# Queues laid by a list scheduler inside the kernel, and gate columns copied with the values

## The chip, the cores and the metric

The kernel runs on one core of one Trainium2 chip. Its time is the device time of one execution in microseconds (us). TensorE (PE) multiplies matrices; VectorE (DVE), ScalarE (ACT) and GpSimd (POOL) work on elements; SyncE (SP) issues loads and stores. Each engine takes its instructions strictly from the front of its own queue, and an instruction that has to wait holds up all that stand behind it.

## The reference

Three stages follow each other, all in float32, for 2 batches of 768 rows.

```
# 1: attention, 8 heads of width 64, window of 96 keys plus 8 global keys
scores = q @ k.T / 8 + bias(head, distance);  scores = where(keep, scores, -1e9)
a = softmax(scores);  x = a @ v                      # heads side by side: 512 wide
# 2: four causal attention experts of width 64, two of four chosen per row
logits = x @ w_gate;  top 2 of 4;  w = softmax over the two chosen
ye = softmax(causal(x wq[e] (x wk[e]).T / 8)) @ (x wv[e]) @ wo[e]
x = sum over chosen e of w[e] * ye
# 3: mixing along the rows (rank 32), then a channel MLP
u = x + (U V mixed over the rows);  out = u + relu(u @ w_ch1) @ w_ch2      # 512 -> 2048 -> 512
```

Four of the weights come as float64 (U, V, w_ch1 and w_ch2) and are narrowed to float32 on the chip with integer operations.

## The kernel before, in words

Stage 1 is cut into 12 pairs of units (`a_pair`), six for each batch, and stage 2 into 12 more (`d_pair`), one for three of the row groups of two experts. A pair goes through `score` (PE, into two banks `S`), `soft` (DVE: the row minimum of the scaled and masked scores, L245; ACT: the exponential with its row sum, L256), `rec` (DVE: reciprocals of the sums, L263 to L266; POOL: the probabilities `pr` times them, L269), `turn` (PE transposes into the banks `T`, `U` or `acc`, L199, and a copy to a tile `pt`, by ACT or DVE in turn), and `values` (PE, into the bank `X`), whose result is copied by ACT as a high part and subtracted by DVE as a low part (`xT`).

The pairs run in positions r = -1 to 23. In position r, PE scores pair r+1, then multiplies the values of pair r-1, then transposes pair r. Between these stand fillers: `c_heads` and `c_values` project x to the experts' queries, keys and values (L362, L363), and `w_fold` multiplies `wo` into a block of w_ch1 (L568). All fillers write into one bank, `acc`, which has one buffer, so each has to be emptied before the next may start. Projections of values put 256 columns of `v` and 4 of gate logits `lg` into that bank; ACT copies `v` (L389) and DVE copies `lg` (L390). From position 6 on the transposes use only `T` and `U`.

A narrowed piece takes an ACT instruction (L83), a POOL instruction that clears all but the sign (L84) and two DVE instructions, here called joins (L89, L90). `w_load` does this for w_ch1 and `w2_load` for w_ch2, whose low part `w2l` DVE then subtracts (L75).

After the pairs comes a seam: `y_turn`, `y_mix` and `y_out` mix along the rows. `y_out` adds the mixed part to `zT` (DVE, L626), copies the sum as a high part (ACT) and subtracts the low part (DVE). The banks `S` are then given to `h`, so the first `h` matmul also waits for all four additions of batch 0. Stage 3 (`M`) is four halves of 16 steps: in each step PE makes a block `h` of the hidden layer, ACT and DVE make its two parts (L649, L650), and PE multiplies the block before it with w_ch2 into three banks. In the first 13 steps DVE still narrows w_ch2.

The order on every engine is the order in which the program is written: `in_order` at the end of `run` chains each instruction to the one before it on its engine. `run` sets what is written when: the table `fill` gives the fillers of each position, `at` and `stages` put loads, conversions and scalings at named points ("dma", "mid", "mid2", "end") of a position, and `position` writes one position out.

Of the kernel before, what the change touches and what calls it, by code (L numbers as in the profile page):

```python
# [9 lines left out]
F32 = mybir.dt.float32  # L10
# [8 lines left out]
P = 128  # L19
# [27 lines left out]

class Pair:
# [6 lines left out]
class Body:  # L55
# [36 lines left out]
    def raw_tile(self):  # L92
        return self.cv.tile([P, 2 * DM], I32, tag="wr", name=self.uid("cr"), bufs=3)
# [107 lines left out]
    def moved(self, t, w, g):  # L201
        pt = self.soft_.tile([P, 512], F32, tag="pt", name=self.uid("pt"), bufs=4)
        (self.hi_dve if g % 2 else self.hi_act)(pt[:, :w], t[:, :w])
        return pt


    def a_load_qk(self, J, first=False):
        nc, a, raw = self.nc, self.a, self.araw
        b, j = divmod(J, NJ)
        qr = raw.tile([P, S], F32, tag="qr", name=self.uid("qr"), bufs=2)  # L210
        kx = raw.tile([P, KW], F32, tag="kx", name=self.uid("kx"), bufs=2)
# [139 lines left out]
    def stacks(self, pool):  # L351
        t = lambda tag, shape, dt: pool.tile(shape, dt, tag=tag, name=self.uid(tag))
        qk = [t(f"qk{n}", [P, 2, S], F32) for n in range(2)]
        v = t("v", [P, NB, E * D], F32)
        g = t("g", [P, NB, E], F32)
        lg = t("lg", [P, NB, E], F32)
        return *qk, v, g, lg
# [20 lines left out]
    def c_values(self, b, t):  # L378
        nc = self.nc
        v, g, lg = self.st[b][2:5]  # L380
# [24 lines left out]
    def gate(self, b):  # L405
        nc = self.nc
        g, lg = self.st[b][3:5]
        sh = [P, NB, E]
        cnt = self.small.tile(sh, F32, tag="cnt", name=self.uid("cnt"), bufs=2)
        c = self.small.tile(sh, F32, tag="cmp", name=self.uid("cmp"), bufs=2)  # L410
        m = self.small.tile([P, NB], F32, tag="gm", name=self.uid("gm"), bufs=2)
# [18 lines left out]
    def causal(self, pool):  # L430
        nc = self.nc
        self.cm = pool.tile([P, 640], F32, name="cm")
        nc.vector.memset(self.cm, 0.0)
# [112 lines left out]
    def w_load(self, f):  # L546
        raws, ts = [], []
        for c in range(0, 4, 2):
# [4 lines left out]
            yield  # L553
# [3 lines left out]
        self.w1[f] = [t.bitcast(F32).rearrange("p (c n) -> p c n", c=2) for t in ts]  # L557
        for r, t in zip(raws, ts):
            self.narrow_join(r, t)
            yield  # L560
# [71 lines left out]
    def M(self, side):  # L632
# [34 lines left out]
        def store(m, t):  # L667
            b, th = halves[m]
            o = self.soft_.tile([P, DM], F32, tag="pt", name=self.uid("o"), bufs=4)
# [93 lines left out]

    def open(self, name, side="left", bufs=1, space=None):
        kw = {"space": space} if space is not None else {"side": side}
        cm = self.tc.tile_pool(name=self.uid(name), bufs=bufs, **kw)
        pool = cm.__enter__()
        self.cms[id(pool)] = cm
        return pool

    def close(self, *pools):
        for p in pools:
            self.cms.pop(id(p)).__exit__(None, None, None)


    def run(self, dense):
        nc = self.nc
        mark = len(nc.cur_bb.bb.instructions)
        self.cms = {}
# [49 lines left out]
        if not dense:  # L829
            for J in range(2, 2 * NJ):  # L830
                r = 3 * (J // 2) + J % 2
                at(r - 2, "dma", self.a_load_qk, J)
                at(r - 2, "end", self.a_scale, J)
                at(r, "dma", self.a_load_v, J)
        for kc in range(4):
            stages(lambda kc=kc: self.wall_load(kc), (kc, "dma"), (kc + 1, "mid"), (kc + 2, "end"))
        uv = [self.u_load, lambda: self.v_load(0), lambda: self.v_load(1)]
        for n, g in enumerate(uv):
            r = 6 + n
            stages(g, (r, "dma"), (r + 1, "mid"), (r + 1, "end"), (r + 2, "mid"), (r + 2, "end"))  # L840
# [9 lines left out]
        fill[6] = [], [], H0[:1]  # L850
        fill[7] = H0[1:2], H0[2:3], []
        fill[8] = H0[3:4], V0[:1], []
        fill[9] = V0[1:2], V0[2:3], []
        fill[10] = V0[3:4], V0[4:5], []
        fill[11] = V0[5:], [], []
        fill[12] = G0[:1], G0[1:2], []
        fill[13] = G0[2:3], G0[3:], []
        fill[14] = H1[:1], H1[1:2], H1[2:3]
        fill[15] = H1[3:], V1[:1], V1[1:2]
        fill[16] = V1[2:3], W[0:1], V1[3:4]  # L860
        fill[17] = V1[4:5], V1[5:], W[1:2]
        fill[18] = G1[:1], G1[1:2], W[2:3]
        fill[19] = G1[2:3], G1[3:], W[3:4]
        fill[20] = [], W[4:5], []
        fill[21] = [], W[5:6], []
        fill[22] = [], W[6:7], []
        at(11, "end", self.gate, 0)
        at(17, "mid2", self.gate, 1)
        for f in range(DFF // CW):
            r = 16 + f  # L870
            stages(lambda f=f: self.w_load(f), (r - 2, "mid2"), (r - 2, "end"), (r - 1, "mid"), (r - 1, "end"))
# [17 lines left out]
        aux.setdefault((14, "dma"), []).insert(0, middle)  # L889
# [14 lines left out]
        def position(r):  # L904
# [4 lines left out]
            full = f1 or f2 or f3 or not pv  # L909
            if nx:  # L910
                nx.score()
            if cur:
                cur.rec()
# [3 lines left out]

            def mins(n):
                for _ in range(n):
                    if next(gen, 1):  # L920
                        break
# [14 lines left out]
            def moved():  # L936
                if outs:
                    outs.pop(0)()

            if not full:  # L940
                mins(6)
                exps(4)
                pv.out_hi()
# [206 lines left out]
```

## Time and profile before

| | us |
|---|---|
| median of 3 runs | 510.98 |
| lowest and highest of them | 509.60, 513.28 |
| the profiled execution's own time | 514.29 |
| its span, first to last instruction | 511.6 |
| PE busy | 459.1 |
| DVE, ACT and POOL busy | 249.3, 201.3, 110.3 |
| mean granted clock of PE | 0.964 |

The profiled execution is one run, 3.3 us above the median of the others; 2.7 us of its time lie outside the span. Matmuls are pipelined and their ends are modelled, so a busy PE need not be PE at its peak. A name such as `acc` stands for all buffers of a tile. L12 is line 12 of the kernel before.

### The profile page before, as it was taken

How to read it: one execution, taken by the hardware profiler on the slowest of the kernel's cores; microseconds unless marked ns; L12 is line 12 of the kernel's file. 1: busy time of each engine (PE TensorE's matmuls, PEld its weight loads, DVE VectorE, ACT ScalarE, POOL GpSimd, SP SyncE). 2: the span in 40 equal slices, each digit the busy share in tenths (PEclk: the TensorE clock that was granted, in tenths of full speed). 3: DMA queues.
4: the chain of work that ended last, by engine and by line, in shares of the span. 5: the costliest groups of instructions: out<-in, count | busy, mean ns of one | idle time of the engine just before them, and what ended most of it. 6: DMA issues, size and time to landing. Idle time of an engine off the chain costs nothing. (4 is left out here: it accounts for less than half of the span.)

```text
span 511.6 us, 7948 instructions
## 1 busy us (share of the span) xinstructions
PE 459.1 (90%) x2916; PEld 384.9 (75%) x2916; DVE 249.3 (49%) x720; ACT 201.3 (39%) x547; POOL 110.3 (22%) x210
## 2 busy tenths in 40 slices
PE   5898799787999977987985999899999999999995
PEld 4676689676887766865774887788888888888883
DVE  4597647556436566465657688941111211111111
ACT  6686557643334444425443444521111111111111
POOL 3577326322231323313421122200000000000000
PEclk9798799989999999998997999999999999999999
DMA  8444622100041221222222333310000100010002
GB/s 301 167 156 156 201 96 77 38 1 1 5 162 41 85 84 41 83 82 85 83 82 83 123 124 124 124 42 21 0 1 0 63 1 0 1 62 1 0 1 69
DMA packets 17648, 36.66 MB, mean 72 GB/s; under 512 B 2560, under 2 KB 6400, under 8 KB 17600
## 3 DMA queue, kind: packets, MB, share of 16 engines
q1 hardware_dynamic: 15728, 34.49, 20.8%
q10 hardware_dynamic: 1872, 1.58, 0.9%
q8 instruction: 25, 0.41, 0.3%
q14 instruction: 23, 0.19, 0.1%
HBM read 32.91 MB, written 3.15 MB: 70 GB/s over the span
## 5 line engine op out<-in xcount | busy, mean ns | idle before, releaser
L256 ACT ACTIVATE pr<-pr,nm 128x256 f32<-128x256 f32 (+4 forms) x144 | 77.4, 540 | 61.3 <-DVE nm L245 61.3
L650 DVE SCALAR_TENSOR_TENSOR pr<-h,pr 128x384 fp32r<-128x384 f32 x64 | 35.5, 554 | 128.3 <-ACT pr L649 128.3
L269 POOL TENSOR_SCALAR pr<-pr,rec 128x256 f32<-128x256 f32 (+4 forms) x144 | 72.0, 521 | 120.2 <-DVE rec L266 66.6
L649 ACT ACTIVATE pr<-h 128x384 fp32r<-128x384 f32 x64 | 31.4, 490 | 136.4 <-PE h L363 136.3
L84 POOL TENSOR_SCALAR cr<-cr 128x512 f32<-128x512 f32 (+2 forms) x35 | 25.4, 733 | 92.6 <-ACT ct L83 76.2
L362 PE MATMUL acc<-xT,wh 128*128 128x384 f32 x128 | 36.2, 365 | 5.5 <-ACT qk L69 5.0
L89 DVE SCALAR_TENSOR_TENSOR cr<-cr 128x512 int32<-128x512 int32 (+2 forms) x35 | 27.8, 794 | 15.1 <-POOL cr L84 15.1
L241 PE MATMUL S<-kx,qr 64*128 64x256 f32 (+1 forms) x192 | 29.3, 448 | 5.8 <-ACT qr L224 4.5
L568 PE MATMUL acc<-ct,woT 128*128 128x256 f32 x128 | 30.4, 392 | 4.3 <-DVE lg L390 2.3
L199 PE MATMUL T<-ident,pr 128*128 128x128 f32 x164 | 28.6, 292 | 5.6 <-POOL pr L269 5.5
L199 PE MATMUL U<-ident,pr 128*128 128x128 f32 x148 | 26.4, 295 | 7.6 <-ACT pt L69 5.6
L245 DVE CUSTOM_DVE_ANT_0 pr<-S,dw 128x256 f32<-128x256 f32 x80 | 29.2, 419 | 6.8 <-PE S L241 5.5
L568 PEld LDWEIGHTS acc<-ct,woT 128*128 128x128 f32 x128 | 24.5, 197 | 8.5 <-DVE lg L390 2.8
L362 PEld LDWEIGHTS acc<-xT,wh 128*128 128x128 f32 x128 | 23.6, 199 | 7.8 <-ACT qk L69 5.8
L241 PEld LDWEIGHTS S<-kx,qr 64*128 64x128 f32 x192 | 20.7, 229 | 11.5 <-ACT qr L224 4.8
L90 DVE SCALAR_TENSOR_TENSOR ct<-ct,cr 128x512 int32<-128x512 int32 (+2 forms) x35 | 26.8, 767 | 1.8
L199 PEld LDWEIGHTS U<-ident,pr 128*128 128x128 f32 x148 | 19.1, 150 | 11.3 <-POOL pr L269 5.6
L72 DVE COPY pt<-T 128x512 f32<-128x512 f32 x26 | 17.9, 688 | 19.6 <-PE T L199 19.5
L199 PEld LDWEIGHTS T<-ident,pr 128*128 128x128 f32 x164 | 20.2, 148 | 9.5 <-POOL pr L269 8.4
L256 ACT ACTIVATION_READ_ACCUMULATOR pr<-pr,nm 128x1 f32 x144 | 27.2, 189 | 0.0
L245 DVE CUSTOM_DVE_ANT_0 pr<-S,cm 128x512 f32<-128x512 f32 (+3 forms) x48 | 24.5, 554 | 3.2 <-PE S L241 3.2
L362 PE MATMUL acd<-w2h,pr 128*128 128x512 f32 x64 | 25.3, 395 | 0.0
(266 smaller groups left out, 1053.7 us busy)
## 6 DMA issues: line engine op xcount, KB each, us to landing
cr<-in_w_dram SPq DMA_DIRECT2D x32, 512.0 KB, 3.6
kx<-in_kx_dram SPq DMA_DIRECT2D x7, 464.0 KB, 5.4
v<-in_v_dram SPq DMA_DIRECT2D x8, 384.0 KB, 3.1
qr<-in_q_dram SPq DMA_DIRECT2D x7, 384.0 KB, 4.1
va<-in_va_dram SPq DMA_DIRECT2D x8, 320.0 KB, 3.5
cr<-in_wall_dram SPq DMA_DIRECT2D x4, 386.0 KB, 5.4
out_dram<-o SPq DMA_DIRECT2D x12, 128.0 KB, 1.7
out_dram<-o ACTq DMA_DIRECT2D x12, 128.0 KB, 1.7
```

What stands on the lines that cost most here:

```text
L84: nc.gpsimd.tensor_scalar(hi.bitcast(F32), hi.bitcast(F32), 0.0, -0.0, op0=ALU.mult, op1=ALU.add)
L89: nc.vector.scalar_tensor_tensor(lo, lo, 29, hi, op0=ALU.logical_shift_right, op1=ALU.bitwise_or)
L90: nc.vector.scalar_tensor_tensor(t, t, 3, lo, op0=ALU.logical_shift_left, op1=ALU.bitwise_or)
L199: self.nc.tensor.transpose(t[:, k * P : (k + 1) * P], s, self.ident)
L241: self.nc.tensor.matmul(sp[:, h, :], q[s], k[s], start=True, stop=True)
L245: self.nc.vector.tensor_tensor_reduce(out=out, in0=sp, in1=mask, scale=scale, scalar=start, op0=ALU.add, op1=ALU.min, accum_out=nm)
L256: self.nc.scalar.activation(pr[:, h, :], pr[:, h, :], AF.Exp, bias=nm[h], scale=-1.0, accum_out=den[:, k, h : h + 1])
L269: nc.gpsimd.tensor_scalar(pr[:, h, :], pr[:, h, :], rec[:, k, h : h + 1], 0.0, op0=ALU.mult, op1=ALU.add)
L362: mm(out, lh, rh, start=first, stop=False), mm(out, lh, rl, start=False, stop=False),
L568: nc.tensor.matmul(ac[:, p, :], self.woT[:, kc, p * P : (p + 1) * P], w1[kc // 2][:, kc % 2, :], start=kc == 0, stop=kc == 3)
L649: nc.scalar.activation(hh, hp, AF.Relu)
L650: nc.vector.scalar_tensor_tensor(hl, hp, 0.0, hh.bitcast(F32), op0=ALU.max, op1=ALU.subtract)
```

## The change

PE keeps the order in which the program is written. The other engines and the queue of loads get an order that a list scheduler computes inside the kernel: `Order.before` reads from the operands which instruction needs which, adds what a buffer's next use and a closed pool need, and keeps PE's order; `Order.length` gives each instruction a nominal length; `Order.queues` goes through the program in simulated order and always takes, among the instructions that could start first, the one with the longest way to the end behind it. `in_order` then chains each engine's queue in that order.

Beside it: the values' copy takes 260 columns at once, by ACT and DVE in turn, and the gate reads its logits from the last four of them; the gate counts with one comparison of all pairs; `cm` is cleared on POOL; raw tiles, `qr` and `kx` get one more buffer, and `pt` is split in two tags of two; loads are written a position earlier; and the fillers of positions 6 to 19 move to about one position earlier.

```diff
-        return self.cv.tile([P, 2 * DM], I32, tag="wr", name=self.uid("cr"), bufs=3)
+        return self.cv.tile([P, 2 * DM], I32, tag="wr", name=self.uid("cr"), bufs=4)
...
+    def length(self, i, e):
...
+        if i.opcode == "DMACopy":
+            return 450, 0, n * outs[0].ap[0][1] * 4
...
+        if e == "Activation":
+            return 150 + 0.87 * n + (120 if len(outs) > 1 else 0), 0, 0
+        if e == "DVE":
+            return (80 + 1.04 * n if i.opcode == "ISA" else 190 if n <= 64 else 150 + 1.06 * n), 40, 0
+        return (130 if n <= 64 else 230 + 0.88 * n), 60, 0
...
+        pe = [k for k, e in enumerate(self.eng) if e == "PE"]
+        for a, b in zip(pe, pe[1:]):
+            self.after[b].add(a)
+
+    def queues(self):
...
+        for _ in range(n):
+            t, e = min((min(max(free[e], ready[k]) for k in s), e) for e, s in open_.items() if s)
+            k = max((k for k in open_[e] if max(free[e], ready[k]) <= t), key=lambda k: (way[k], -k))
+            open_[e].discard(k)
+            line[e].append(k)
+            end = free[e] = t + self.cost[k]
...
-        def out():
-            nc.scalar.activation(v[:, t, :], ac[:, :256], AF.Copy)
-            nc.vector.tensor_copy(lg[:, t, :], ac[:, 256:260])
-        return out
+        return lambda: (self.hi_dve if t % 2 else self.hi_act)(v[:, t, :], ac)
...
-        for e in range(E):
-            le = lg[:, :, e : e + 1].to_broadcast((P, NB, E))
-            if e:
-                nc.vector.tensor_tensor(c[:, :, :e], lg[:, :, :e], le[:, :, :e], ALU.is_ge)
-            nc.vector.tensor_tensor(c[:, :, e:], lg[:, :, e:], le[:, :, e:], ALU.is_gt)
-            nc.vector.tensor_reduce(cnt[:, :, e : e + 1], c, axis=AX.X, op=ALU.add)
+        nc.vector.tensor_tensor(over[:, :, :, 0, :], other, own, ALU.is_gt)
+        nc.vector.tensor_tensor(over[:, :, :, 1, :], other, own, ALU.is_equal)
+        nc.vector.tensor_tensor(over[:, :, :, 1, :], over[:, :, :, 1, :], self.earlier.unsqueeze(1).to_broadcast(full), ALU.mult)
+        nc.vector.tensor_reduce(cnt.unsqueeze(3), over.rearrange("p t e k n -> p t e (k n)"), axis=AX.X, op=ALU.add)
...
-        fill[6] = [], [], H0[:1]
-        fill[7] = H0[1:2], H0[2:3], []
-        fill[8] = H0[3:4], V0[:1], []
...
-        fill[19] = G1[2:3], G1[3:], W[3:4]
...
+        fill[6] = [], H0[:1], H0[1:2]
+        fill[7] = H0[2:3], H0[3:], []
+        for n in range(3):
+            fill[8 + n] = V0[2 * n : 2 * n + 1], V0[2 * n + 1 : 2 * n + 2], []
...
+        fill[18] = G1[2:3], G1[3:], W[2:3]
+        for n in range(4):
+            fill[19 + n] = [], W[3 + n : 4 + n], []
...
-        last = {}
-        for i in self.nc.cur_bb.bb.instructions[mark:]:
-            e = i.engine
-            if e in last:
+        ins = [
+            (n, i) for n, i in enumerate(self.nc.cur_bb.bb.instructions)
+            if n >= mark and (Order.aps(i.outs) or Order.aps(i.ins))]
+        for queue in Order(self, ins).queues().values():
+            for a, b in zip(queue, queue[1:]):
                 self.tc.add_manual_dep(
-                    i, last[e].name,
+                    b, a.name,
                     mybir.DependencyInfo(mybir.DependencyClass.NoSync, mybir.DependencyReason.DATA), reason="order")
-            last[e] = i
```

DVE's queue where position 10 begins: the copies of position 9's last transposes (`pt`), then the minima of the pair scored in position 10 (`ISA`, with `dw` as the mask). Before:

```order
L390 COPY lg_113<-acc_1293 128x4
L72 COPY pt_1320<-T_1313 128x512
L75 TENSOR_TENSOR vs<-ct_1156,vs 32x384
L89 SCALAR_TENSOR_TENSOR cr_1057<-cr_1057 96x384
L90 SCALAR_TENSOR_TENSOR ct_1290<-ct_1290,cr_1057 96x384
L263 TENSOR_SCALAR rec_1339<-den_1235 128x8
L264 RECIPROCAL rec_1339<-rec_1339 128x8
L245 ISA pr_1365,nm_1367<-S_1329,dw 128x256
```

The same place in the change:

```order
L416 TENSOR_SCALAR rec_1366<-den_1249 128x8
L417 RECIPROCAL rec_1366<-rec_1366 128x8
L225 COPY pt_1303<-T_1295 128x512
L225 COPY v_111<-acc_1309 128x260
L225 COPY pt_1335<-T_1328 128x512
L398 ISA pr_1377,nm_1379<-S_1341,dw 128x256
```

The joins of `V` and the subtraction of its low part are gone from here to earlier in the queue, the reciprocals stand ahead of the copies, and the values' copy includes the gate columns.

DVE's queue at the seam: the low part `zs` of the mixed rows, the additions to `zT`, the subtractions `y00l` and `y01l`, and the narrowing of w_ch2. Before:

```order
L75 TENSOR_TENSOR zs_2989<-S_2917,zs_2989 32x256
L75 TENSOR_TENSOR wol<-cr_2887,woh 128x1024
L89 SCALAR_TENSOR_TENSOR cr_2889<-cr_2889 128x512
L90 SCALAR_TENSOR_TENSOR ct_2966<-ct_2966,cr_2889 128x512
L626 TENSOR_TENSOR zT_98<-zT_98,S_2916 128x384
L75 TENSOR_TENSOR y00l<-zT_98,y00h 128x384
L626 TENSOR_TENSOR zT_98<-zT_98,S_2916 128x384
L75 TENSOR_TENSOR y00l<-zT_98,y00h 128x384
L626 TENSOR_TENSOR zT_98<-zT_98,S_2917 128x384
L75 TENSOR_TENSOR y01l<-zT_98,y01h 128x384
L626 TENSOR_TENSOR zT_98<-zT_98,S_2917 128x384
L75 TENSOR_TENSOR y01l<-zT_98,y01h 128x384
```

In the change:

```order
L242 SCALAR_TENSOR_TENSOR cr_2868<-cr_2868 128x512
L228 TENSOR_TENSOR wpl<-acc_2933,wph 128x2x256
L243 SCALAR_TENSOR_TENSOR ct_2945<-ct_2945,cr_2868 128x512
L228 TENSOR_TENSOR zs_2968<-S_2896,zs_2968 32x256
L242 SCALAR_TENSOR_TENSOR cr_2948<-cr_2948 128x512
L783 TENSOR_TENSOR zT_98<-zT_98,S_2895 128x384 x2
L228 TENSOR_TENSOR w2l_3014<-ct_2945,w2h_3013 128x512
L783 TENSOR_TENSOR zT_98<-zT_98,S_2896 128x384 x2
L228 TENSOR_TENSOR y00l<-zT_98,y00h 128x384 x2
```

`wol` and the first piece's joins stand further ahead, the four additions come in two couples with one subtraction of w_ch2 between them, and the subtractions `y01l` have moved far back.

DVE's queue in the first steps of stage 3 in the change: `pr` is the second part of a hidden block, `z` the low part of batch 1's rows.

```order
L807 SCALAR_TENSOR_TENSOR pr_3044<-h_3037,pr_3044 128x384
L228 TENSOR_TENSOR w2l_3078<-ct_2980,w2h_3077 128x512
L243 SCALAR_TENSOR_TENSOR ct_3019<-ct_3019,cr_2983 128x512
L242 SCALAR_TENSOR_TENSOR cr_3022<-cr_3022 128x512
L243 SCALAR_TENSOR_TENSOR ct_3083<-ct_3083,cr_3022 128x512
L228 TENSOR_TENSOR w2l_3117<-ct_3019,w2h_3116 128x512
L242 SCALAR_TENSOR_TENSOR cr_3086<-cr_3086 128x512
L228 TENSOR_TENSOR w2l_3163<-ct_3083,w2h_3162 128x512
L228 TENSOR_TENSOR z_3069<-T_3070,z_3068 128x512
L807 SCALAR_TENSOR_TENSOR pr_3095<-h_3088,pr_3095 128x384
```

Three pieces of w_ch2 get their low part between the first two hidden blocks; in the kernel before, one does.

## Rows read from the trace of the kernel before

**Rows 1.** The page's first part: busy us, share of the span, instructions.
```profile
PE 459.1 (90%) x2916; PEld 384.9 (75%) x2916; DVE 249.3 (49%) x720; ACT 201.3 (39%) x547; POOL 110.3 (22%) x210
```
**Rows 2.** Windows by stage: length, busy us (instructions) by engine, clock, DMA share, GB/s.
```profile
51.84:255.80 203.96, 176.93 (x1392) 148.93 (x1392) 118.33 (x402) 98.88 (x286) 62.53 (x114) 0.96 0.24 72
255.80:277.27 21.47, 13.39 (x118) 11.06 (x117) 13.64 (x24) 8.27 (x18) 4.84 (x7) 0.92 0.30 98
277.27:326.99 49.72, 47.52 (x223) 39.38 (x224) 39.48 (x60) 23.47 (x47) 10.65 (x12) 0.97 0.35 117
```
**Rows 3.** PE's waits: instruction, what ended them, us in total, times, longest us.
```profile
PE acc L362 <- DVE lg L390: 6.6, 4, 2.1
PE h L362 <- DVE zT L626: 6.1, 1, 6.1
PE U L199 <- ACT pt L69: 5.6, 4, 2.8
PE T L199 <- POOL pr L269: 5.5, 6, 2.9
PE acc L362 <- ACT qk L69: 5.0, 3, 2.5
...
PE acc L568 <- DVE lg L390: 2.3, 2, 1.8
PE acc L362 <- DVE w2l L75: 2.1, 3, 0.9
PE acc L568 <- DVE qk L72: 2.0, 2, 1.0
PE U L199 <- POOL pr L269: 2.0, 4, 0.8
```
**Rows 4.** Timeline of position 10: start, us, engine, line, operation [idle before <-releaser].
```profile
95.45 0.55 DVE L89 SCALAR_TENSOR_TENSOR cr<-cr 96x384 int32<-96x384 int32 x1
...
96.83 0.37 DVE L245 CUSTOM_DVE_ANT_0 pr<-S,dw 128x256 f32<-128x256 f32 x1
...
97.31 0.51 ACT L256 ACTIVATE pr<-pr,nm 128x256 f32<-128x256 f32 x1 [2.94 <-DVE nm L245]
...
99.64 0.60 PE L199 MATMUL T<-ident,pr 128*128 128x128 f32 x4
...
101.73 0.36 ACT L389 ACTIVATE v<-acc 128x256 f32<-128x256 f32 x1
...
102.13 0.16 DVE L390 COPY lg<-acc 128x4 f32<-128x4 f32 x1 [1.54 <-ACT v L389]
...
102.35 0.39 PE L362 MATMUL acc<-wh,xT 128*128 128x260 f32 x1 [2.11 <-DVE lg L390]
```
**Rows 5.** Sum over windows at clock 0.50: 45.02:48.43, 58.67:65.5, 103.04:106.46, 126.94:130.35, 239.58:242.99.
```profile
sum 20.48, PE 19.64 PEld 17.01 DVE 5.71 ACT 8.01 POOL 5.91; mean PE 3.93 PEld 3.40 DVE 1.14 ACT 1.60 POOL 1.18
```
**Rows 6.** Timeline of the seam.
```profile
268.69 1.23 DVE L75 TENSOR_TENSOR wol<-cr,woh 128x1024 fp32r<-128x1024 f32 x1
...
269.32 1.12 POOL L84 TENSOR_SCALAR cr<-cr 128x512 f32<-128x512 f32 x1 [1.99 <-issue]
269.84 1.16 DVE L89 SCALAR_TENSOR_TENSOR cr<-cr 128x512 int32<-128x512 int32 x1
...
271.63 0.55 DVE L626 TENSOR_TENSOR zT<-zT,S 128x384 f32<-128x384 f32 x1
...
276.47 0.55 DVE L626 TENSOR_TENSOR zT<-zT,S 128x384 f32<-128x384 f32 x1
```
**Rows 7.** Timeline of PE in stage 3: first matmul of steps 1, 12 and 13.
```profile
284.43 0.42 PE L362 MATMUL h<-y00h,wph 128*128 128x384 f32 x1
...
326.99 0.34 PE L362 MATMUL h<-y00h,wph 128*128 128x384 f32 x1
...
330.13 0.34 PE L362 MATMUL h<-y00h,wph 128*128 128x384 f32 x1
```
**Rows 8.** The first join: count, shortest, median and longest ns, first and last start.
```profile
L89 DVE SCALAR_TENSOR_TENSOR cr<-cr x35: 349/689/1156, 75.6 to 333.3; 128x512 int32<-128x512 int32 x32, 96x384 int32<-96x384 int32 x2, 128x192 int32<-128x192 int32 x1
```

More of the change, by code (lines that the diff above doesn't have):

```diff
@@ L431, in causal @@
         nc = self.nc
+        self.earlier = pool.tile([P, E, E], F32, name="earlier")
+        nc.gpsimd.memset(self.earlier, 0.0)
+        for e in range(1, E):
+            nc.gpsimd.memset(self.earlier[:, e, :e], 1.0)
         self.cm = pool.tile([P, 640], F32, name="cm")
-        nc.vector.memset(self.cm, 0.0)
+        nc.gpsimd.memset(self.cm, 0.0)
         nc.gpsimd.affine_select(
@@ L839, in run @@
             r = 6 + n
-            stages(g, (r, "dma"), (r + 1, "mid"), (r + 1, "end"), (r + 2, "mid"), (r + 2, "end"))
+            stages(g, (r, "dma"), (r + 1, "mid"), (r + 2, "a"), (r + 2, "mid"), (r + 3, "a"))
         at(7, "end", self.causal, const)
@@ L916, in position @@
             gen = nx.soft() if nx else iter(())
[L918 to L921, printed above, removed]
+            if not full:
+                next(gen, None), next(gen, None)
+            if cur:
+                cur.rec()
+            for _ in gen:
+                pass
+            if not full:
+                do(r, "a")
             def exps(n):
@@ L934, in turn, with moved, filler, out @@
                         outs.append(turns.pop(0)())
-            def moved():
-                if outs:
-                    outs.pop(0)()
+            def moved(n=1):
+                for _ in range(n):
+                    if outs:
+                        outs.pop(0)()
+            def filler(fs):
+                return [fn() for fn in fs]
+            def out(ev):
+                for e in ev:
+                    e()
             if not full:
-                mins(6)
-                exps(4)
-                pv.out_hi()
+                exps(6)
+                if pv:
+                    pv.out_hi()
                 turn(2)
                 moved()
-                mins(1)
-                moved()
-                turn(1)
-                mins(99)
-                exps(2)
-                pv.out_lo()
+                exps(99)
+                if pv:
+                    pv.out_lo()
                 moved()
@@ L954, in position @@
                 moved()
+                turn(1)
                 do(r, "mid")
-                exps(99)
+                do(r, "mid2")
+                moved()
                 do(r, "end")
                 return
-            mins(99)
-            exps(4)
+            exps(2)
+            do(r, "sign")
+            do(r, "a")
+            exps(3)
             if pv:
@@ L1058, in turn1 @@
         def turn1(n):
-            z = [self.soft_.tile([P, 512], F32, tag="pt", name=self.uid("z"), bufs=4) for x in "hl"]
+            z = [self.soft_.tile([P, 512], F32, tag=f"pt{x}", name=self.uid("z"), bufs=2) for x in range(2)]
             self.y_turn(1, 2 * n, z, self.bank("TU"[n % 2]))()
```

233 lines of the change are left out of this document (172 added, 61 removed).

## Prediction

> **What bounds the kernel now.** I began with the page's busy times: TensorE (PE) is busy for 90% of the span and the next, VectorE, for 49% [rows 1]. So the kernel ends when PE ends, and a change that leaves PE's instructions as they are can only win what PE spends waiting or at half clock. The table of stages says where that is [rows 2]. The long middle, positions 6 to 22 with attention, the second stage and all filler, lasts 204 us with 27.0 idle. The seam between the second stage and the last is 21.5 us with 8.1 idle. The first stretch of the last stage is 49.7 us with 2.2 shown idle, and there VectorE (DVE) is busy for 39.5 us, the one place where PE has a rival for the bound. Behind 327 us a step of that stage takes 3.14 [rows 7], and I count nothing there.
>
> The list of PE's waits then says what ends them [rows 3]. Three kinds carry nearly all. Filler matmuls wait for their only accumulator bank to be emptied: 6.6 and 5.0 before `acc` matmuls of the projections, 2.3 and 2.0 before the folds, 15.9 together. Transposes wait for a copy out of their bank or for GpSimd's (POOL) normalised rows: 5.6, 5.5 and 2.0, 13.1 together. The first `h` waits once for 6.1. None of these engines is full; what they owe PE stands behind something else in their own queue.
>
> One position shows how [rows 4]. While PE is at the next pair's scores, DVE is at two joins of a matrix that is needed much later, the first at 95.45, and its first minimum starts at 96.83. So ScalarE's exponentials start late, at 97.31, the copy of `v`, queued behind all eight, starts at 101.73, the copy of `lg`, which reads the same bank, at 102.13, and the next group into `acc` at 102.35, after 2.11 us of waiting. From 103.04 on the granted clock is 0.50.
>
> The clock is the second half of the cost. Five stretches at 0.50, the lower of the two levels, 1.2 GHz, lie between 45 and 243 us, and PE is busy in them for 19.64 us [rows 5]. At 2.4 GHz the same work takes half, so 9.8 us are lost. The one at 103.04 begins 0.7 us after the wait shown in rows 4 ended; I take the others to have the same cause.
>
> **The change, part by part.** PE has as many instructions as before, in the order in which the program is written. Positions 6 to 18 get their filler about one place earlier, so its matmuls cost the same; what changes is the queues that serve PE.
>
> *Accumulator waits.* Of 15.9 us I take 11 back. In the first place shown, minima now follow the last copy directly, without joins ahead of them, and `v` with the gate columns is one copy instead of a copy on ScalarE and a second on DVE. Eight transposes lie between two fillers, and the second four of them alone took 0.60 at 99.64. That covers a copy of 0.36 which is at the head of its queue, but not one that has to wait for an exponential (0.51) first, so I don't take all. Bounds: 5 (only the waits of the kind in rows 4 go) and 15.9.
>
> *Transpose waits.* Of 13.1 I take 7, since half is behind a queue (the copy to `pt` placed behind exponentials) and half is GpSimd's own pace, which no order changes. Bounds 2 and 13.1.
>
> *Clock.* With these waits gone, most of the five stretches go: 6 of 9.8. Bounds 0 and 9.8.
>
> *Seam.* DVE does the `wol` subtraction (1.23), a join (1.16) and its second half (0.69) before the first `zT` addition, then alternates additions with subtractions that each wait for ScalarE; the last addition starts at 276.47 [rows 6], and PE's first `h`, after its 6.1 of waiting, at 277.27, where the stage begins [rows 2, 3]. Between the start of the first addition and the end of the last lie 5.4 us, of which the four additions themselves are 2.2. Now the additions stand together ahead of the subtractions, so most of the other 3.2 goes, and the 1.23 of `wol` is done earlier; one join and one `w2l` subtraction (priced as the 0.69 half) still stand in the way. 3.2 + 1.2 − 0.7 is 3.7, and I take 4, since the chance of a shorter join beside an idle GpSimd is on this side; bounds 2 and 5.
>
> *First pass of the last stage.* From 284.43 to 326.99 are eleven steps, 42.56 us, against 3.14 for a step once nothing is in its way (326.99 to 330.13) [rows 7]: 8.0 too long. Part of that is PE's own side work, which stays, and 2.1 is shown as waiting for `w2l` [rows 3]. The joins now run up to three pieces ahead, with four raw buffers instead of three. I take 3; bounds 0 and 5.
>
> *Edits at nothing.* Twelve `lg` copies of 0.16 go; six `v` copies move from ScalarE to DVE; the gate has 12 DVE instructions instead of 19. In the middle stage DVE is busy for 118 of 204 us and ScalarE for 99 [rows 2], and that idle time covers them; their worth is counted in the accumulator waits. The `cm` mask and the new `earlier` tile go to GpSimd's start, where it waits for the first loads anyway. Loads are issued earlier, but SyncE's queue has w1 loads in front of late `v` and `va` loads; those are needed a position later. If one came late, the next values would wait for its landing; PE's list has no wait for a load in this stage today.
>
> *What comes back.* Shorter positions leave each pair's chain (minima, exponentials, reciprocal, normalising, transposes) less slack. The nearest row is a transpose's wait for GpSimd, 5.5 over 6 times, 0.9 each. If each of the 17 positions from 6 to 22 got one more it would be 15; if none, 0. I take 4, nearer to none: minima and exponentials of a pair take 4.9 (96.83 to 101.73), and a position lasts 12.0 on average now (204 over 17) and 10.6 with 24 us gone, so the rest of the chain keeps some 5.7.
>
> Sum: 11 + 7 + 6 + 4 + 3 − 4 = 27. The first five attention positions, which have no filler, are left at nothing. The span goes from 511.6 to 484.6; the profiled run was 514.3, 2.7 more than its span, and the median of the runs is 511.0, 3.3 less than that run. So 487.3 for a run like the profiled one, **484 us** for the median. With all best ends the sum is 49 (462 us), with all worst ends −6 (517).
>
> **Rivals.**
> *Queues frozen on wrong lengths, slower.* The order is fixed from nominal lengths, with PE at full clock. Place: ScalarE's and DVE's queues in positions 6 to 22, where copies for PE now stand between exponentials. If PE comes later than laid down, a copy waits at the head of its queue, the exponentials behind it wait too, the next pair's transposes come late, and PE falls to half clock again. Price of one: 2.8, the longest wait of transposes for `pt` [rows 3], and 2.0, half of a mean stretch at 0.50 (20.48 over five) [rows 5], 4.8 together. It takes 32 us to turn 484 into over 516, so it decides from 7 of the 17 positions on; with eight, 522 us. For it: five positions pay such a price today with a fixed order. Against it: a later PE also delays what feeds on it, so the order mostly stays right.
>
> *Conversions collide, a smaller gain.* Joins and sign-clearing instructions are pulled forward side by side. A join beside GpSimd's sign clearing took 1.16, and that one 1.12 [rows 6]; the median over all 35 joins is 0.69 [rows 8]. If all 32 wide joins paid the difference of 0.47, DVE would have 15 us more, most of it where PE waits for DVE, in the folds and the first pass. With 13 of it on the path: 497 us. In the Trainium skill, "SBUF — State Buffer", section "Who interferes with whom", a VectorE instruction with two SBUF inputs contends with a GpSimd instruction that reads SBUF, which speaks against putting both kinds of work forward together. By that rule the nominal lengths are too short wherever the two meet, and the 1.16 beside 1.12 agrees with it; that the median join met nothing in this trace is why I give it little.
>
> *Nothing happens.* PE is 90% busy, its order is fixed, and the waits just move: 511 us.
>
> **How the numbers follow.** Forecast, 464 to 495 us: 0.70. Collisions, 495 to 505: 0.14. Nothing, 506 to 516: 0.08. Frozen queues, over 516: 0.08. A measurement tells about 1% (5 us) from no change, so faster 0.84, same 0.08, slower 0.08. The range takes in the first two and stops at the third: 464 to 506, leaving out some 0.16 above and a few hundredths below.
>
> **What would show it.** In the new profile PE's waits before `acc` should total under 6 us and those of transposes under 8; the granted clock should be 0.50 in at most two stretches between 45 and 250 us; the first `h` should come within 3 us of the last `S` matmul; the eleven steps should take under 40 us. With 24 of the 27 ahead of it, the last stage begins near 253 instead of 277. I am wrong if PE's waits keep their total and only change their names, or if DVE's joins grow towards 1.1 us on average.

## The result, and the profile after

The changed kernel takes 465.8 us (median of four runs, 465.5 to 466.5) against 511.5 for the kernel before (509.6 to 513.3): ratio 0.911, 95% interval 0.907 to 0.915. It is faster, by more than I said: 45.7 us where the forecast had 27 (484 us). The profiled run took 465.9 us and its span is 464.1, against 511.6: 47.5 us to account for.

From here on, L numbers are lines of the kernel whose trace is shown. The page's first part of the kernel after (busy us, share of the span, instructions):

```profile
PE 442.0 (95%) x2916; PEld 375.7 (81%) x2916; DVE 244.6 (53%) x699; ACT 201.1 (43%) x541; POOL 120.7 (26%) x215
```

PE has the same 2916 instructions and 17.1 us less busy time than in [rows 1]; as its work has not changed, most of this has to be clock (12.7 is worked out below). Its idle time fell from 52.5 to 22.1, the other 30.4.

Windows of the kernel after by stage (length, busy us and instructions of PE, PEld, DVE, ACT and POOL, granted clock, DMA share, GB/s); the second to fourth answer to [rows 2], cut at the same instructions of PE, the first is everything ahead of position 6:

```profile
0.00:49.23 49.23, 39.94 (x345) 29.93 (x345) 40.70 (x166) 38.20 (x133) 36.31 (x85) 0.97 0.75 256
49.23:219.65 170.42, 166.34 (x1391) 142.25 (x1391) 115.99 (x382) 97.14 (x277) 67.04 (x111) 1.00 0.25 78
219.65:235.21 15.56, 13.17 (x119) 11.07 (x117) 10.50 (x18) 9.82 (x21) 5.71 (x8) 1.00 0.32 101
235.21:279.34 44.13, 44.13 (x223) 38.36 (x224) 42.89 (x72) 25.78 (x49) 11.65 (x12) 1.00 0.41 132
```

Against [rows 2] the middle lost 33.5 us (204.0 to 170.4), the seam 5.9, the first pass of the last stage 5.6; ahead of position 6 it is 2.6 (51.84 to 49.23), and behind the twelfth step 0.2 more (184.6 to 184.8). The sum is 47.5, rounded. In the middle PE's idle time went from 27.0 to 4.1 and its clock from 0.96 to 1.00. In the first pass PE is now never idle, and VectorE is busy for 42.9 of 44.1: what was a rival for the bound is close to being it.

PE's waits in the kernel after (instruction, what ended them, us, times, longest):

```profile
PE U L352 <- POOL pr L422: 2.0, 2, 1.5
PE acc L513 <- ACT qk L222: 1.9, 3, 0.9
PE h L513 <- ACT y01h L222: 1.3, 1, 1.3
...
PE acc L513 <- ACT v L222: 0.8, 2, 0.4
PE T L352 <- POOL pr L422: 0.5, 2, 0.3
PE acc L513 <- DVE v L225: 0.5, 1, 0.5
PE acc L513 <- DVE qk L225: 0.4, 1, 0.4
PE acc L725 <- DVE qk L225: 0.4, 1, 0.4
```

The projections' and folds' waits before `acc` (L513, L725) add up to 4.0, where the rows of [rows 3] that I counted had 15.9; transposes into U and T have 2.5 in these rows and 0.4 in a smaller one, from 13.1. The wait for `lg` is gone with its copy, that for `zT` has become 1.3 for `y01h`, that for `w2l` is gone. The longest wait of PE in the middle is now 0.9.

The same place of a position as [rows 4], from the kernel after (start, us, engine, line, operation, idle before and releaser):

```profile
87.20 0.69 DVE L225 COPY pt<-T 128x512 f32<-128x512 f32 x1 [0.44 <-PE T L352]
88.39 0.42 DVE L398 CUSTOM_DVE_ANT_0 pr<-S,dw 128x256 f32<-128x256 f32 x1 [0.49 <-POOL pr L422]
...
88.86 0.51 ACT L409 ACTIVATE pr<-pr,nm 128x256 f32<-128x256 f32 x1 [1.43 <-DVE nm L398]
...
92.69 0.60 PE L352 MATMUL T<-ident,pr 128*128 128x128 f32 x4
...
93.29 0.36 ACT L222 ACTIVATE v<-acc 128x260 f32<-128x260 f32 x1
...
93.70 0.39 PE L513 MATMUL acc<-wh,xT 128*128 128x260 f32 x1 [0.41 <-ACT v L222]
```

PE's scores of this pair start at 87.10, the first minimum follows at 88.39, 1.3 later; before it was 94.04 and 96.83, 2.8 later, with a subtraction and two joins of a conversion between. The copy of `v` still stands behind all eight exponentials, so nothing put it at the head of its queue; the exponentials are just done 1.5 us sooner, and 2.11 us of waiting have become 0.41.

### The profile page after: what moved, and what is told of

Its sections match the earlier page's. It is cut to its first block, busy times and chain, and to the rows that moved or that the text cites. A ratio compares the mean times of both kernels' runs of the same rounds, so it can differ in the third digit from the quotient of the medians.

```text
span 464.1 us, 7933 instructions
## 1 busy us (share of the span) xinstructions
PE 442.0 (95%) x2916; PEld 375.7 (81%) x2916; DVE 244.6 (53%) x699; ACT 201.1 (43%) x541; POOL 120.7 (26%) x215
## 4 chain that ended last, share of the span: by engine, by line
PE 78%; ACT 8%; POOL 5%; DVE 4%; issue 3%; DMA 1%; ACTq 0%; DVEq 0%; POOLq 0%
PE h L513 10%; PE acc L513 9%; PE acd L513 7%; PE S L394 6%; PE acc L725 6%; ACT pr L409 5%; PE h L514 5%; POOL pr L422 4%; PE acc L514 4%; PE X L513 4%; PE X L652 4%; PE T L513 4%; PE acd L514 4%; PE U L513 3%; PE U L352 2%
## 5 line engine op out<-in xcount | busy, mean ns | idle before, releaser
L422 POOL TENSOR_SCALAR pr<-pr,rec 128x256 f32<-128x256 f32 (+4 forms) x144 | 78.8, 567 | 93.5 <-DVE rec L419 68.2
L237 POOL TENSOR_SCALAR cr<-cr 128x512 f32<-128x512 f32 (+2 forms) x35 | 27.4, 788 | 49.3 <-ACT ct L236 38.8
L513 PE MATMUL acc<-xT,wh 128*128 128x384 f32 x128 | 34.4, 349 | 1.9 <-ACT qk L222 1.9
L394 PE MATMUL S<-kx,qr 64*128 64x256 f32 (+1 forms) x192 | 25.6, 402 | 4.8 <-ACT qr L377 4.5
L725 PE MATMUL acc<-ct,woT 128*128 128x256 f32 x128 | 29.1, 380 | 0.4 <-DVE qk L225 0.4
L236 ACT ACTIVATE ct<-cr 128x512 f32<-128x512 f32 (+2 forms) x35 | 22.9, 658 | 14.0 <-PE acc L725 10.9
L352 PE MATMUL T<-ident,pr 128*128 128x128 f32 x164 | 26.3, 279 | 0.9 <-POOL pr L422 0.5
L725 PEld LDWEIGHTS acc<-ct,woT 128*128 128x128 f32 x128 | 23.7, 190 | 3.6 <-DVE qk L225 0.7
L242 DVE SCALAR_TENSOR_TENSOR cr<-cr 128x512 int32<-128x512 int32 (+2 forms) x35 | 25.7, 734 | 1.6 <-POOL cr L237 1.5
L394 PEld LDWEIGHTS S<-kx,qr 64*128 64x128 f32 x192 | 18.6, 203 | 9.3 <-ACT qr L377 4.9
L513 PEld LDWEIGHTS acc<-xT,wh 128*128 128x128 f32 x128 | 22.2, 188 | 3.9 <-ACT qk L222 2.6
L513 PE MATMUL acd<-w2h,pr 128*128 128x512 f32 x64 | 25.3, 395 | 0.0
L513 PE MATMUL acd<-w2l,pr 128*128 128x512 f32 x64 | 25.3, 395 | 0.0
L514 PE MATMUL acd<-w2h,pr 128*128 128x512 f32 x64 | 25.3, 395 | 0.0
## 6 DMA issues: line engine op xcount, KB each, us to landing
kx<-in_kx_dram SPq DMA_DIRECT2D x7, 464.0 KB, 4.7
```

The lines of the kernel that those rows point to most:

```text
L237: nc.gpsimd.tensor_scalar(hi.bitcast(F32), hi.bitcast(F32), 0.0, -0.0, op0=ALU.mult, op1=ALU.add)
L242: nc.vector.scalar_tensor_tensor(lo, lo, 29, hi, op0=ALU.logical_shift_right, op1=ALU.bitwise_or)
L352: self.nc.tensor.transpose(t[:, k * P : (k + 1) * P], s, self.ident)
L394: self.nc.tensor.matmul(sp[:, h, :], q[s], k[s], start=True, stop=True)
L422: nc.gpsimd.tensor_scalar(pr[:, h, :], pr[:, h, :], rec[:, k, h : h + 1], 0.0, op0=ALU.mult, op1=ALU.add)
L513: mm(out, lh, rh, start=first, stop=False), mm(out, lh, rl, start=False, stop=False),
```

## The experiments

What each run's stages took, from the windows of its trace, cut at the same instructions (position 6, the seam's first transpose of `zT`, called its first turn, the first `h`, the twelfth step), in us, beside the median of its runs:

| kernel | median | to position 6 | to first turn | seam | first pass |
|---|---|---|---|---|---|
| before | 511.5 | 51.8 | 206.4 | 19.1 | 49.7 |
| text_only | 498.2 | 51.4 | 190.9 | 17.7 | 50.3 |
| sched_only | 477.1 | 51.9 | 180.2 | 12.8 | 44.3 |
| merge_only | 507.6 | 49.7 | 199.8 | 19.1 | 50.0 |
| sched_merge | 475.0 | 52.1 | 178.4 | 12.9 | 44.3 |
| after | 465.8 | 49.2 | 173.0 | 13.0 | 44.1 |
| after_again | 465.9 | 49.4 | 173.0 | 13.0 | 44.2 |
| pool_sp_text | 464.0 | 48.7 | 171.9 | 12.8 | 44.3 |
| flat_lengths | 476.0 | 49.1 | 174.0 | 16.2 | 50.3 |
| text_first | 473.1 | 52.9 | 173.7 | 14.2 | 45.5 |
| double_norm | 482.8 | 58.6 | 179.4 | 14.5 | 44.3 |
| wide_signal | 467.9 | 49.9 | 170.7 | 13.8 | 45.8 |

Each row is one trace. The second trace of the changed kernel repeats every stage within 0.2 us. But merge_only is 2.1 us shorter ahead of position 6, which its edit doesn't reach: the stretch at half clock that the kernel before has at 45 us [rows 5] is missing there. A difference of some 2 us in that first stage is therefore not safely the work of an edit.

My theory: the gain comes from the queues that the scheduler lays. The first rival: it comes from the new text (fills, buffers, the merged copy). The first four runs part the two.

**text_only.** The changed program, each engine in the order of the text:

```diff
-        for queue in Order(self, ins).queues().values():
-            for a, b in zip(queue, queue[1:]):
-                self.tc.add_manual_dep(b, a.name, ...)
...
+        for i in self.nc.cur_bb.bb.instructions[mark:]:
+            e = i.engine
+            if e in last:
+                self.tc.add_manual_dep(i, last[e].name, ...)
+            last[e] = i
```

> The changed program with its new text (fills, buffers, one copy of values with gate columns), every engine in the order in which the text is written; the list scheduler is not used. Theory (the queues laid by the scheduler bring the gain): 495 to 512 us, waits of PE before acc and before transposes together still above 20 us, three or more stretches at half clock between 45 and 250 us. Rival (the new text brings it, the scheduler little): under 480 us, those waits under 12 us.

Measured 498.2 us (496.9 to 500.3), ratio 0.972, 0.968 to 0.977. Its waits of PE:

```profile
PE h L513 <- DVE zT L783: 6.0, 1, 6.0
...
PE acc L513 <- ACT qk L222: 3.9, 4, 1.9
PE acc L513 <- DVE v L225: 3.5, 1, 3.5
PE acc L725 <- DVE qk L225: 3.3, 1, 3.3
...
PE acc L513 <- DVE w2l L228: 2.0, 3, 0.8
```

The time is as the theory had it. The waits for `acc` are 11.9 (10.7 in these rows) and those of transposes, in smaller ones, 9.4: 21.3, just above my 20. But only two stretches at half clock, not three, are left between 45 and 250 us. The waits for `zT` (6.0) and `w2l` (2.0) stand as before; in the table the first pass is as long as before, the seam 1.4 shorter.

**sched_only.** The kernel before with the classes `Room` and `Order` and the new `in_order`, nothing else:

```diff
...
-        for i in self.nc.cur_bb.bb.instructions[mark:]:
...
+        for queue in Order(self, ins).queues().values():
```

> The kernel before with its old text, fills, buffers and copies, and only the queues of ScalarE, VectorE, GpSimd and SyncE laid by the list scheduler. Theory (the scheduler brings the gain): 466 to 480 us, waits of PE before acc and transposes together under 12 us. Rival (the text brings it): 495 us or more.

Measured 477.1 us (477.0 to 478.0), ratio 0.931, 0.928 to 0.933. The waits of PE:

```profile
PE U L352 <- POOL pr L422: 2.8, 3, 1.6
PE acc L515 <- DVE lg L543: 2.3, 3, 1.1
PE acc L515 <- DVE qk L225: 2.2, 3, 1.1
...
PE h L515 <- ACT y01h L222: 1.2, 1, 1.2
```

Against the 512.2 of the kernel before, measured beside it, the scheduler alone brings 35 us and the text alone 14, where both together bring 46. The scheduler alone brings all that seam and first pass gain; in the middle either brings a part (26 us the one, 15 the other, 33 both). The time is as the theory had it, with a share for the text that I had put at nothing by itself. Its sign is missed: all waits before `acc` and of transposes are 6.7 and 8.1 (the list has smaller rows than these), 14.8 together and not under 12, where the changed kernel, counted in the same way, has 7.9.

**merge_only.** Kernel before, one copy for `v` and gate columns:

```diff
-        def out():
-            nc.scalar.activation(v[:, t, :], ac[:, :256], AF.Copy)
-            nc.vector.tensor_copy(lg[:, t, :], ac[:, 256:260])
-        return out
+        return lambda: (self.hi_dve if t % 2 else self.hi_act)(v[:, t, :], ac)
```

> The kernel before with one edit: v and the gate columns leave their bank in one copy, on ScalarE and VectorE in turn. Theory (a copy waits for its place in the queue, whatever its number): 503 to 512 us, since a copy still stands behind eight exponentials or two joins. Rival (the second copy of the same bank is what PE waits for, 6.6 + 2.3 us in the list of waits): those two lines fall below 2 us and the time to 496 to 502 us.

Measured 507.6 us (505.3 to 509.5), ratio 0.991, 0.987 to 0.994: a gain of 3 to 7 us, inside the theory's range and short of the rival's. Its waits where the copy is concerned:

```profile
PE acc L565 <- DVE v L72: 2.2, 1, 2.2
...
PE acc L362 <- DVE v L72: 1.4, 2, 0.8
PE acc L362 <- ACT v L69: 1.2, 1, 1.2
```

The 8.9 that stood at `lg` have become 5.2 at `v` (4.8 in these rows, 0.4 in a smaller one), not under 2 as the rival had it. So some 3.7 of that wait went with the second copy; the rest I put down to the place of the one copy in its queue, which this run doesn't show by itself.

**sched_merge.** The same edit in sched_only.

> The kernel before with its queues laid by the scheduler and with one copy for v and the gate columns; fills, buffers and the rest of the text as before. What of the 11 us between the scheduler alone (477) and the changed kernel (466) is the copy, what the fills and buffers? Theory (the second copy of the bank is a wait of its own, 2.3 us in the waits of the scheduler alone, and merging it gave 4.6 us without the scheduler): 472 to 475 us. Rival (the fills and buffers are worth nothing, as I costed them): 465 to 468 us. Third (the scheduler hides the second copy anyway): 476 to 478 us.

Measured 475.0 us (473.5 to 476.2), ratio 0.926, 0.920 to 0.932, against 0.931, 0.928 to 0.933, for sched_only: these intervals overlap, so 2 us for the copy is not certain. What is left to the changed kernel, 9.2 us by the medians, is then fills, buffers and the rest of the text: 2.9 ahead of position 6, 5.4 in the middle. I had costed the moved fills at nothing for their own matmuls; they were not tried one by one.

**pool_sp_text.** The changed kernel, GpSimd and SyncE in the order of the text:

```diff
-        pe = [k for k, e in enumerate(self.eng) if e == "PE"]
-        for a, b in zip(pe, pe[1:]):
-            self.after[b].add(a)
+        for fixed in ("PE", "Pool", "SP"):
+            pe = [k for k, e in enumerate(self.eng) if e == fixed]
+            for a, b in zip(pe, pe[1:]):
+                self.after[b].add(a)
```

> The changed kernel, but GpSimd and SyncE keep the order of the text, and only ScalarE and VectorE are laid by the scheduler. Theory (PE's waits hang on ScalarE and VectorE alone): 464 to 470 us, PE's waits for GpSimd's rows within 2 us of the changed kernel's 2.5. Rival (the sign clearings and the loads moved ahead matter too): 475 us or more, with PE waiting for pr of GpSimd or for loads.

Measured 464.0 us (463.9 to 464.2), ratio 0.904, 0.902 to 0.907. Laying GpSimd's and SyncE's queues brings nothing; VectorE's and ScalarE's are the gain. PE waits for GpSimd's rows 2.2 us, as the theory had it. The time is 1.8 us below the changed kernel's and the best here; its interval ends where that of the changed kernel begins (0.907 in one set of runs, 0.904 in another), so it is no slower, and hardly shown to be faster.

The next two ask what in the scheduler counts, against the rival of queues frozen on wrong lengths.

**flat_lengths.**

```diff
-        if e == "Activation":
-            return 150 + 0.87 * n + (120 if len(outs) > 1 else 0), 0, 0
-        if e == "DVE":
-            return (80 + 1.04 * n if i.opcode == "ISA" else ...), 40, 0
-        return (130 if n <= 64 else 230 + 0.88 * n), 60, 0
+        return 500, 0, 0
```

> The changed kernel with wrong nominal lengths: every instruction of ScalarE, VectorE and GpSimd counts 500 ns when the queues are laid, whatever its size; PE's and the loads' lengths stay. Theory (an order that is a little wrong costs little, since a later PE also delays what feeds on it): 465 to 473 us. Rival (queues frozen on wrong lengths make PE wait): 4.8 us for each position hit, 485 us or more, with half-clock stretches back.

Measured 476.0 us (473.7 to 476.2), ratio 0.929, 0.923 to 0.935. The waits of PE from the first turn of `zT` to the twelfth step:

```profile
PE acc L510 <- DVE pr L803: 3.1, 5, 1.0
PE S L776 <- DVE zs L224: 2.8, 1, 2.8
```

The time is between the two, and the place tells why: the middle, where VectorE has room, takes 1.0 us more, the seam 3.2 and the first pass 6.2. Behind position 6 one stretch at half clock came back, in the seam, as the 2.8 for `zs` ends. Wrong lengths cost in the first pass, where VectorE is nearly full, and in the seam, where PE waits for a single chain, not in the positions that the rival named.

**text_first.**

```diff
-            k = max((k for k in open_[e] if ...), key=lambda k: (way[k], -k))
+            k = max((k for k in open_[e] if ...), key=lambda k: -k)
```

> The changed kernel; among the instructions that are ready at the earliest moment the scheduler takes the one that comes first in the text, instead of the one with the longest way to the end. Theory (what counts is that nothing unready stands ahead of something ready, the choice among the ready ones is second): 465 to 474 us. Rival (the priority by the longest way puts PE's copies first): 480 us or more, waits of PE before acc and transposes over 15 us.

Measured 473.1 us (472.9 to 474.4), ratio 0.926, 0.920 to 0.932. The theory holds: the rule that an engine takes what is ready, in the order of the text, keeps all but 7 us of 46. The priority by the longest way is worth those, 3.6 of them ahead of position 6.

**late_bank and later_bank** ask whether PE's waits are what pulls its clock down. The copy of a piece of `v` is done six times, then twelve times (for the even pieces of the first batch):

```diff
-        return lambda: (self.hi_dve if t % 2 else self.hi_act)(v[:, t, :], ac)
+        def out():
+            for _ in range(6 if b == 0 else 1):
+                (self.hi_dve if t % 2 else self.hi_act)(v[:, t, :], ac)
+        return out
```

> The changed kernel with the copy of v out of its bank done six times instead of once for the six pieces of the first batch (positions 8 to 10); five copies of 0.37 to 0.43 us hold the bank some 2 us longer, six times. Theory (a wait of that kind pulls the clock down behind it): six waits of PE before acc of 1 to 2 us, and stretches at half clock appear between 66 and 110 us, which cost as much again: 475 to 490 us. Rival (the clock has another cause): the waits alone, 472 to 478 us, and no stretch at half clock there.

Measured 472.5 us (471.6 to 474.2), 6.6 above the changed kernel's 465.9, measured beside it. The three waits, then the first and the last of four windows around them:

```profile
77.73 0.39 PE L513 MATMUL acc<-wh,xT 128*128 128x260 f32 x1 [2.17 <-ACT v L222]
88.13 0.39 PE L513 MATMUL acc<-wh,xT 128*128 128x260 f32 x1 [1.92 <-ACT v L222]
98.77 0.39 PE L513 MATMUL acc<-wh,xT 128*128 128x260 f32 x1 [1.92 <-ACT v L222]
```

```profile
66.00:78.00 12.00, 9.21 (x84) 8.18 (x85) 9.53 (x32) 8.89 (x30) 8.46 (x16) 1.00 0.71 231
...
99.00:110.00 11.00, 10.77 (x88) 9.32 (x88) 9.15 (x34) 7.10 (x23) 3.74 (x8) 1.00 0.01 1
```

Three waits came, not six, and the clock stayed at 1.00 in all four windows, though one of 2.11 in [rows 4] had a fall behind it. The three are those behind ScalarE's copies. This run spoke for the rival; the next was made to decide.

> The changed kernel with the copy of v on ScalarE done twelve times for the three even pieces of the first batch (positions 8 to 10). Three waits of PE before acc of about 4.2 us (six copies gave 2.2, 1.9 and 1.9; six more of 0.37 add 2.2 each). Theory (a wait pulls the clock down behind it, but one of about 2 us not every time): a stretch at half clock behind each of the three, 2 us each on top of 12.6 us of waiting: 482 to 487 us. Rival (the clock falls for another cause, as the run with six copies, 6.6 us longer without any such stretch, would have it): the waits alone, 477 to 480 us, no stretch there.

Measured 484.7 us (484.3 to 485.6). The three waits, and the stretches at 0.50, the lower level, 1.2 GHz:

```profile
80.34 0.59 PE L513 MATMUL acc<-wh,xT 128*128 128x260 f32 x1 [4.70 <-ACT v L222]
95.88 0.59 PE L513 MATMUL acc<-wh,xT 128*128 128x260 f32 x1 [4.98 <-ACT v L222]
112.39 0.58 PE L513 MATMUL acc<-wh,xT 128*128 128x260 f32 x1 [5.03 <-ACT v L222]
```

```profile
78.00:84.80 6.80, 4.46 (x20) 4.27 (x20) 0.43 (x1) 3.21 (x8) 1.47 (x4) 0.50 0.04 16
95.10:101.90 6.80, 6.02 (x26) 5.46 (x28) 1.12 (x2) 1.57 (x4) 0.00 (x0) 0.50 0.01 2
112.10:115.50 3.40, 3.11 (x14) 3.11 (x15) 0.11 (x1) 0.72 (x2) 0.00 (x0) 0.51 0.00 0
```

Each of the three has a fall that begins while PE still waits. PE is busy for 13.6 us at half clock there; half of it, 6.8, I count as lost, on top of 14.7 of waiting, where the changed kernel has 0.8. That makes 20.7; the spans differ by 19.7 (483.8 and 464.1), the medians by 18.9. So these long waits of PE took the clock with them. Length alone doesn't decide below that: the wait of 3.5 in text_only's rows above, which ended at 160.54, left the clock at 1.00 all through the window below, while one of 1.9 that ended at 191.74 had a fall behind it at 193.1.

```profile
157.00:167.00 10.00, 6.54 (x55) 5.47 (x56) 6.72 (x16) 2.09 (x6) 1.38 (x3) 1.00 0.34 107
```

**double_norm** asks how much room the pair's chain has, of which I had let 4 us come back:

```diff
                 nc.gpsimd.tensor_scalar(pr[:, h, :], pr[:, h, :], rec[:, k, h : h + 1], 0.0, op0=ALU.mult, op1=ALU.add)
+                self.hi_pool(pr[:, h, :], pr[:, h, :])
```

> The changed kernel with every normalising instruction of GpSimd followed by a second one that multiplies the same rows by one: 144 more of 0.57 us, some 4.6 us for each pair of heads. Theory (the pair's chain has slack, so nothing of the gain came back): 466 to 474 us, waits of PE for GpSimd's rows under 8 us. Rival (the chain is near the bound, and GpSimd's pace sets the transposes): 485 us or more, waits for its rows over 20 us.

Measured 482.8 us (479.7 to 483.8), ratio 0.939, 0.933 to 0.945, between the two. Windows up to position 6, and from there to the last transposes of the second stage:

```profile
0.00:58.58 58.58, 44.98 (x345) 33.00 (x345) 36.13 (x161) 38.06 (x134) 46.15 (x126) 0.85 0.53 193
58.58:237.90 179.32, 171.34 (x1427) 145.80 (x1426) 124.40 (x388) 98.57 (x277) 120.87 (x214) 0.99 0.26 83
```

In the middle GpSimd does 51 us more than in the changed kernel (120.9 against 69.6) and the stretch takes 6.4 longer: there the chain has the room that I gave it. Ahead of position 6, where no filler covers it, 10 us more on GpSimd go with 9.4 more in time, a part of it clock (0.85, from 0.97). PE's waits for GpSimd's rows are 10.8, between the 8 and the 20 named, and 3.0 of them stand in the middle.

**wide_signal.** pool_sp_text with 300 ns instead of 70 from engine to engine:

```diff
-    SIGNAL, LAND, ISSUE, RATE = 70, 400, 1300, 300.0
+    SIGNAL, LAND, ISSUE, RATE = 300, 400, 1300, 300.0
```

> The kernel with GpSimd and SyncE in the order of the text, and 300 ns instead of 70 counted for the way from one engine to another when the queues are laid. Theory (small errors in the lengths cost little, either way): within 3 us of that kernel's 464. Rival (more room before each step takes the last short waits away): 460 us or less.

Measured 467.9 us (466.6 to 468.2), 3.9 above that kernel. The middle became 1.2 shorter, the seam 0.9, the start 1.2 and the first pass 1.5 longer, so neither expectation held, and 70 is the better of the two.

**after_again** is the changed kernel once more, the yardstick of the three runs beside it.

> The changed kernel once more, on the chip on which the other three run, as their yardstick: 464 to 468 us by every theory.

Measured 465.9 us (464.4 to 466.5).

## Why the prediction was right, and where its sizes were off

The 465.8 us lie inside the range of 464 to 506, but only 1.8 above its lower end and 18 below the forecast of 484. Place and mechanism were right in the main; that the range still held the size owes something to luck, for all six terms of the sum erred to the same side.

**The bound and the place** were right: PE's instructions are as many, and the whole gain is PE's waits and clock. Of the signs named, the waits (4.0 and 2.9), the clock (no stretch at 0.50 between 45 and 250 us) and the first `h` (1.3 us behind the last `S` matmul) came out as said; the last stage begins at 235.2, well ahead of the 253.

**Accumulator waits**, 11 taken back: 11.9 measured (15.9 to 4.0). The mechanism was half right. In the place shown the minima do follow at once; but the copy didn't move to the head of its queue, the queue ahead of it got done earlier. merge_only shows the share of the second copy.

**Transpose waits**, 7: 10.2 (13.1 to 2.9). The step that failed is "half is GpSimd's own pace, which no order changes". The longest of these waits in the kernel before:

```profile
230.67 0.18 ACT L256 ACTIVATION_READ_ACCUMULATOR pr<-pr,nm 128x1 f32 x1
...
233.02 1.12 DVE L89 SCALAR_TENSOR_TENSOR cr<-cr 128x512 int32<-128x512 int32 x1 [3.49 <-POOL cr L84]
...
236.78 0.16 DVE L263 TENSOR_SCALAR rec<-den 128x4 f32<-128x4 f32 x1
...
237.53 2.70 POOL L269 TENSOR_SCALAR pr<-pr,rec 128x768 f32<-128x768 f32 x4 [3.92 <-DVE rec L266]
...
238.49 0.33 PE L199 MATMUL T<-ident,pr 128*128 128x128 f32 x1 [2.86 <-POOL pr L269]
```

The last row sum is there at 230.9, but a join that isn't ready holds VectorE up for 3.49 us; it then does this join, three more conversion instructions and a subtraction before it starts the reciprocals at 236.78; GpSimd is idle for the last 3.92 before it gets them. So its lateness is a queue's too, here VectorE's. In the kernel after, GpSimd's normalising instructions are no faster (567 ns on average, from 521), and PE waits for none of its rows in the middle.

**Clock**, 6 of 9.8: this was the worst-sized term. All five stretches of [rows 5] went, 9.8. And I had left out two others of the kernel before that were in sight:

```profile
14.30:21.10 6.80, 5.67 (x26) 3.63 (x26) 2.89 (x12) 3.41 (x15) 3.54 (x10) 0.50 0.15 60
273.70:280.50 6.80, 3.23 (x9) 3.06 (x10) 5.00 (x10) 3.42 (x7) 1.19 (x1) 0.50 0.15 59
```

The second began while PE waited for the first `h` and cost the first steps of the last stage 1.6; the first, 2.8, is in the changed kernel a stretch of 3.4 us at 13.1 that costs 1.5. Together 9.8 + 1.6 + 1.3 is 12.7, twice my 6. That waits cause it was an assumption in the prediction. In the kernel before, each of the five falls begins during a wait or within 1.4 us of its end (waits of 1.2, 2.8, 2.1, 2.5 and 2.9), but waits of 1.5 to 2.1 at four other places had none behind them. later_bank shows it for three waits of 4.7 to 5.0 us; what decides for the shorter ones, up to the 3.5 of text_only, stays open.

**Seam**, 4: the wait for the first `h` fell by 4.8, the window by 5.9, and sched_only has it all. The additions in the kernel after:

```profile
232.14 1.02 DVE L783 TENSOR_TENSOR zT<-zT,S 128x384 f32<-128x384 f32 x2
...
233.93 1.02 DVE L783 TENSOR_TENSOR zT<-zT,S 128x384 f32<-128x384 f32 x2
```

They stand in pairs, 2.8 from the first start to the last end, where [rows 6] have 5.4.

**First pass**, 3: eleven steps take 38.3 (241.00 to 279.34), from 42.6 [rows 7], a gain of 4.2, under the 40 that I had named.

```profile
241.00 0.42 PE L513 MATMUL h<-y00h,wph 128*128 128x384 f32 x1
...
279.34 0.33 PE L513 MATMUL h<-y00h,wph 128*128 128x384 f32 x1
```

**What comes back**, −4: nothing did. PE waits for GpSimd's rows 2.5 in all, for none in the middle, and double_norm shows the room that is left there.

Sum of the measured terms: 11.9 + 10.2 + 12.7 + 4.8 + 4.2 is 43.8 of 47.5; the other 3.7 was not taken apart, beyond a wait of 1.3 for `qr` ahead of position 6 and one of 0.5 for `wpl` in the middle, both gone. Against my 27 the difference is 6.7 in the clock, 4 in what comes back, 3.2 in the transposes, 2.9 in the other three, and that rest. I had discounted waits and clock one by one, the first three terms by 31 to 47%. But most of them have one cause, a queue that holds an unready instruction ahead of a ready one: sched_only takes 35 of the 46 us from all of them at once, and with the new text the result lies close to the sum of all best ends, 49.

**The rivals.** *Frozen queues*: of the five positions said to pay that price today, one lies ahead of position 6 and has a wait of 1.2, not 2.8. In the kernel after, no wait of PE in the middle exceeds 0.9 us, and even with all lengths at 500 ns the middle stays at 174; a wrong order costs in the seam and the first pass instead. *Collisions*: the first join's median is 687 ns, from 689 [rows 8], and its mean fell:

```profile
L242 DVE SCALAR_TENSOR_TENSOR cr<-cr 128x512 int32<-128x512 int32 (+2 forms) x35 | 25.7, 734 | 1.6 <-POOL cr L237 1.5
```

It was 794 ns, 27.8 us. Four of the 35 take over 0.9 us, from ten, and each of these fourteen runs beside a GpSimd instruction. The rule of the Trainium skill, "SBUF — State Buffer", section "Who interferes with whom", that I weighed there isn't contradicted, since such long joins exist in both traces; the new order just doesn't make more of them. *Nothing happens* fell with the time.

## What to carry to other kernels

Where the bounding engine waits for helpers that are half idle, look for what stands unready ahead of ready work in their queues. Here most waits, and the half clock behind some of them, came from that one cause and went together, so don't discount them one by one. Queues laid by "take what is ready" brought 39 of the 46 us on the new text; right lengths mattered most where a helper is nearly full. The new text (moved filler, buffers and one copy, not tried apart but for the copy) was worth another third of what the scheduler brought alone, 11 on 35 us, so judge text and order together.

## What the runs showed of the hardware that I had not expected

The fall of the granted clock began during a long wait of PE, not only behind it: in later_bank at 95.1, with the wait ending at 95.88, and in the kernel before at 273.7, with PE idle until 277.27. The matmul of 260 columns that ends such a wait took 0.59 us against 0.39 at the upper level. And the length of a wait does not tell alone whether a fall follows: 2.11 had one in the kernel before and 1.86 in text_only, while 2.17 in late_bank and 3.46 in text_only had none; the six waits of 4.70 to 6.17 behind earlier matmuls (three in later_bank, one before the first `h` each in before, text_only and merge_only) all had one.
